# Windowed attention and a squared-ReLU layer: crossbar transposes a row ahead, results through GpSimd's queue, loads of rows 1 and 2 held for their turn, zero products in TensorE's gaps

## The chip, the core and the metric

The kernel runs on one core of a Trainium2 chip. The metric is the device time of one execution in microseconds (us). A core has five engines with queues of their own, each worked off in order: TensorE (PE, matrix products), VectorE (DVE), ScalarE (ACT), GpSimd (POOL) and SyncE (SP, which here only issues transfers). An instruction that waits holds up all that stand behind it in its queue. Transfers (DMA) are issued from SP, ACT or POOL.

## The reference

Two steps are computed. The first is attention on q, k, v of shape 8 x 8 x 576 x 64 (batch rows, heads, positions, head width) with a window: heads 0 to 3 see the last 32 positions ("sliding"), heads 4 to 7 every fourth of the last 128 ("dilated"). The second takes the result as 4608 tokens of width 512 through two layers.

```python
mask_plain = (rel >= 0) & (rel < window)
mask_dil = (rel >= 0) & (rel < window * dilation) & (rel % dilation == 0)
...
attn = np.exp(scores)
attn = attn / (np.sum(attn, axis=-1, keepdims=True) + 1e-09)
return np.matmul(attn, v).astype(np.float32)
...
h = x @ w_in
r = np.maximum(h, 0.0)
g = r * r
return (g @ w_out).astype(np.float32)
```

x is 4608 x 512, w_in 512 x 2048, w_out 2048 x 512; the output is 4608 x 512 in float32.

## The kernel before

The order of every engine's instructions is the order of the program text (manual scheduling); buffers come from pools, and a tile waits for its slot to come free.

**Loads.** For each batch row, q and k of the sliding heads go to `sq` (L89, from SP), v to `sv` in six pieces (L96) and `sd` in two (L105), all in float32. GpSimd casts q and k to `nq` (`cast_sliding_qk`, L146, four instructions) and v to `vp` and `vd` (L158, L162; three and four). The staging buffers exist once, so the load of a row waits for the casts of the row before. For rows 0 and 1, q and k of the dilated heads are loaded with a cast, from GpSimd's queue, to `nd` (L117).

**Getting q and k transposed.** Rows 0 and 1 do it on TensorE (`t_sliding` L330, `t_dilated` L344; six products into a PSUM tile, which VectorE copies out for k and ScalarE for q, L142 and L144 in `copy`). Rows 2 to 7 do it by transfers: GpSimd's queue casts the dilated q and k from DRAM to a DRAM buffer `dd` (L175), SP writes `nq` to a DRAM buffer `dp` (L183), and SP issues four crossbar transposes that write `QKTp` and `QKTd` (L192). These two buffers exist once.

**Attention of a row.** Scores: `s_sliding` (L365) and `s_dilated` (L382), two of each, take two PSUM pairs (`pa`, two buffers); ScalarE takes the exp of each of the eight tiles to `AT` and VectorE multiplies by a 0/1 mask (`softmax`, L361). Values: `attn_values` (L497) has seven groups of products (L414, L429), each normalized by VectorE (L401) and then transposed by TensorE (L443, L460) and copied by ScalarE to `xT`.

**The two layers.** The tokens go in nine chunks of 512. `mm1_gen` (L244) makes 16 tiles `ph` of four products each (128x128 by 128x512), ScalarE applies the ReLU (`rt`), VectorE squares (`g`). `mm2_gen` (L277) makes four tiles `po` of 16 products each; `store` (L272) copies each to `ot` (three buffers) on ScalarE and writes it from SP's queue. `mm2_by_rows_gen` (L287), for chunk 0, goes through w_out in four parts so that it can start before all of w_out is there. The four PSUM buffers `pm` are shared by `ph`, `po` and the transposes.

**How the two are mixed.** Chunk b - 1 is computed during row b. The generators stop after every second product, and `pump(n)` (L312) runs n such pieces (two products each). A chunk has 32 pieces of the first layer and 32 of the second. Row 0 runs alone (L519 to L531). Row 1 pumps 6 pieces, issues its loads and w_out's, pumps 26, then mixes its attention with the second layer (L537 to L563). Each row from 2 on (L566 to L579) first issues the casts, the `dp` write and the crossbar transposes of its own row, then the loads of the next, then pumps 24 pieces ahead of its scores (4 pieces after each), and 2 after each step of its values. The memsets at L538, L539, L550 and L551 write a few elements of the staging buffers on VectorE, so that a load that follows waits for VectorE to get there. Chunks 7 and 8 come last, with no attention beside them (L580). w_in is loaded in three parts (L123).

Of the kernel before, what the change touches and what calls it, by code (L numbers as in the profile page):

```python
# [13 lines left out]
P = 128  # L14
# [3 lines left out]
def kernel(  # L18
# [91 lines left out]
    def load_v(b):  # L110
        load_sliding_v(b)
        load_dilated_v(b, nc.sync)

    def dilated_buffer(b):
        return natp.tile([QB, 2, 2, 12 * D], FP16, name=f"nd{b}", tag="nd")
# [5 lines left out]
                nc.gpsimd.dma_start(out=nd[48 * e : 48 * (e + 1), i, :, :], in_=s4[e])  # L121

    def load_w_in():  # L123
        for f0, f1 in ((0, 512), (512, 1024), (1024, 2048)):
            nc.gpsimd.dma_start(
                out=wi[:, :, f0:f1],
                in_=moe_w_in[:, f0:f1].rearrange("(dh dl) f -> dl dh f", dl=P),
            )
# [26 lines left out]
                )  # L155
        return n

    def cast_sliding_v():  # L158
        for m in range(0, NB, 2):
            nc.gpsimd.tensor_copy(vp[:, m : m + 2, :, 0:D], sv[:, m : m + 2, :, :])  # L160

    def cast_dilated_v():  # L162
        for t in range(2):
            for c in range(0, DIL, 2):
                nc.gpsimd.tensor_copy(  # L165
                    vd[:, t, c : c + 2, :, 0:D],
                    sd[:, t, :, D * c : D * (c + 2)].rearrange("p h (c d) -> p c h d", d=D),
                )
# [29 lines left out]
    load_sliding_qk(0, (nc.sync, nc.scalar))  # L198
    reli = const.tile([P, QB], I16, name="reli")
    nc.gpsimd.iota(reli, pattern=[[1, QB]], base=0, channel_multiplier=-1)  # L200
    make_identity(nc, ident)
    nds = {0: dilated_buffer(0)}
    load_dilated_qk(0, nds[0])
    nc.vector.memset(sv[0:PADP, 0, :, :], 0.0)
    nc.vector.memset(sd[0:64, 0, :, :], 0.0)
    load_sliding_v(0)
    load_dilated_v(0, nc.scalar)
    warm = const.tile([P, 1], FP32, name="warm")
    nc.vector.memset(warm, 0.0)
    nc.scalar.activation(warm, warm, ACTF.Exp)  # L210

    relf = const.tile([P, QB], FP32, name="relf")
    nc.vector.tensor_copy(relf, reli)
    lo_ = const.tile([P, QB], FP16, name="lo_")
# [57 lines left out]
    def store(c, t, po):  # L272
        ot = osb.tile([P, DM], FP32, name=f"ot{c}_{t}", tag="ot")
        nc.scalar.copy(ot, po)  # L274
        nc.sync.dma_start(out=out[(c * 4 + t) * P : (c * 4 + t + 1) * P, :], in_=ot)

    def mm2_gen(c, g):  # L277
        for t in range(TOKC // P):
            po = pmool.tile([P, DM], FP32, name=f"po{c}_{t}", tag="pm")
            for ffc in range(NFF):  # L280
                mm2(c, g, po, t, ffc)
                if ffc % 2 == 1 and ffc < NFF - 1:
                    yield
            store(c, t, po)
            yield
# [16 lines left out]
    def hidden(c):  # L302
        return gp.tile([P, NFF, TOKC], FP16, name=f"g{c}", tag="g")

    def moe_gen(c):
        g = hidden(c)
        yield from mm1_gen(c, g)
        yield from mm2_gen(c, g)

    pending: list = []  # L310

    def pump(n):  # L312
        for _ in range(n):
            while pending:
                try:
                    next(pending[0])
                    break
                except StopIteration:
                    pending.pop(0)
# [21 lines left out]
            p_[:, 0:UW].rearrange("x (j p) -> x p j", j=6),  # L341
        )

    def t_dilated(b, n, g, i, wide=False):  # L344
        p_ = pt(f"pd{b}_{g}_{i}", wide)
        for j in range(6):
            nc.tensor.transpose(
                p_[:, QB * j : QB * (j + 1)],
                n[:, i, g, P * j : P * (j + 1)],
                ident[0:QB, 0:QB],  # L350
            )
        for a in range(2):
            copy(
                nc.vector if i else nc.scalar,
                QKTd[:, i, a, KPAD + 2 * g * CL : KPAD + 2 * (g + 1) * CL].rearrange(
                    "x (h p s) -> x h p s", h=2, s=3
                ),
                p_[:, 0:UW].rearrange("x (s a h p) -> x a h p s", a=2, h=2, p=48)[:, a],
            )
# [115 lines left out]
            py[:, 0:UW].rearrange("x (c r i) -> x c i r", c=2, r=DIL),  # L475
        )

    def transposes(b, nq, nd, gap):
        wide = gap == 0
        for hp in range(2):  # L480
            for i in (1, 0):
                t_sliding(b, nq, hp, i, wide)
                pump(gap)
        for g in range(2):
            for i in (1, 0):
                t_dilated(b, nd, g, i, wide and not i)
                pump(gap)

    def attn_scores(b, gap):
        for hp in range(2):  # L490
# [3 lines left out]
            s_dilated(b, g)  # L494
            pump(gap)

    def attn_values(b, gap, wide=False):  # L497
        xs = []
        for mp in range(3):
            xs.append(av_sliding(b, mp))  # L500
            pump(gap)
        x_sliding(b, 0, xs, wide)
        pump(gap)
        ys = [av_dilated(b, 0, 0)]
        pump(gap)
        x_sliding(b, 1, xs, wide)
        pump(gap)
        ys.append(av_dilated(b, 0, 1))
        pump(gap)
        zs = []  # L510
        for a in range(2):
            zs.append(av_dilated(b, 1, a))
            pump(gap)
        x_dilated(b, 0, ys, wide)
        pump(gap)
        x_dilated(b, 1, zs, wide)


    nq = cast_sliding_qk(0, (nc.scalar, nc.scalar, nc.vector, nc.gpsimd))  # L519
    cast_sliding_v()  # L520
    load_w_in()
    cast_dilated_v()
    for hp in range(2):
        for i in (1, 0):
            t_sliding(0, nq, hp, i)
        s_sliding(0, hp)
    for g in range(2):
        for i in (1, 0):
            t_dilated(0, nds[0], g, i)
        s_dilated(0, g)  # L530
    attn_values(0, 0)  # L531


    g0 = hidden(0)
    pending.append(mm1_gen(0, g0))
    pump(6)
    nds[1] = dilated_buffer(1)  # L537
    nc.vector.memset(sq[:, :, :, 0:1], 0.0)  # L538
    nc.vector.memset(nds[1][:, :, :, 0:1], 0.0)  # L539
    load_sliding_qk(1)  # L540
    load_dilated_qk(1, nds[1])
    load_w_out()
    nq = cast_sliding_qk(1, (nc.gpsimd,) * 4)
    pump(26)
    pending.append(mm2_by_rows_gen(0, g0))
    for hp in range(2):
        for i in (1, 0):
            t_sliding(1, nq, hp, i, True)
            pump(1)
    nc.vector.memset(sv[:, 1, :, 0:1], 0.0)  # L550
    nc.vector.memset(sd[:, 1, :, 0:1], 0.0)  # L551
    load_v(1)
    cast_v()
    load_sliding_qk(2)
    load_v(2)
    dd = keep_dilated_qk(2)
    for g in range(2):
        for i in (1, 0):
            t_dilated(1, nds[1], g, i, True)
            pump(1)  # L560
    attn_scores(1, 3)
    attn_values(1, 1, True)
    pump(1000)  # L563


    for b in range(2, B):  # L566
        pending.append(moe_gen(b - 1))
        nq = cast_sliding_qk(b, (nc.gpsimd,) * 4)
        dp = keep_sliding_qk(b, nq)
        transpose_by_dma(dp, dd)  # L570
        cast_v()
        if b + 1 < B:
            load_sliding_qk(b + 1)
            load_v(b + 1)
            dd = keep_dilated_qk(b + 1)
        pump(24)
        attn_scores(b, 4)
        attn_values(b, 2)
        pump(1000)  # L579
    for c in range(B - 1, NTOKC):  # L580
        pending.append(moe_gen(c))
# [31 lines left out]
```

The softmax here doesn't subtract the row's maximum and nothing guards it: scores larger than these inputs give would overflow.

## Time and profile before

| what | us |
|---|---|
| median of 2 runs (343.63 to 344.74) | 344.19 |
| the profiled execution's own time | 343.5 |
| its span in the profile | 341.7 |
| TensorE busy | 303.1 |
| ScalarE, VectorE, GpSimd busy | 171.0, 155.2, 74.8 |
| row 0 (to the first product of the first layer) | 0 to 28.9 |
| rows 1 and 2 | 28.9 to 113.6 |
| rows 3 to 7 | 113.6 to 282.8 |
| chunks 7 and 8 | 282.8 to 338.2 |
| last copy and store | 338.2 to 341.7 |

The page of a profile lists busy times of the engines, which say how full an engine is but not what it waits for; a busy TensorE is a modelled time, because products overlap. The chain of waits follows the work that ended last back to what released each step. The view of waits sums, for each engine and line, the idle time ahead of it and what ended it. A table of stretches gives the busy time of every engine between two times; a row of the batch begins where TensorE turns to the next chunk's first layer.

### The profile page before, as it was taken

The page shows a single profiled execution, that of the slowest core. Times are in us where ns is not written, and L with a number is a line of the kernel's source. Part 1 is how long each engine was busy: PE and PEld are TensorE (multiplying, and loading weights), DVE is VectorE, ACT ScalarE, POOL GpSimd, SP SyncE. Part 2 cuts the span into 40 slices and gives each one's busy share as a digit, 9 for nine tenths or more (in the row PEclk, how much of TensorE's full clock was granted, in tenths as well). Part 3 has the DMA queues.
Part 4 walks back from the last instruction along what each step waited for, and adds up shares of the span by engine and source line. Part 5 has one row for each costly group of instructions (what it writes and reads, how often), then busy time and mean ns, then how long its engine had stood idle before and what let it go on. Part 6 is the DMA issues. An engine that isn't in the chain of part 4 may idle for free.

```text
span 341.7 us, 6096 instructions
## 1 busy us (share of the span) xinstructions
PE 303.1 (89%) x2368; PEld 151.8 (44%) x2368; DVE 155.2 (45%) x354; ACT 171.0 (50%) x292; POOL 74.8 (22%) x119
## 2 busy tenths in 40 slices
PE   0669979938699979998999799979999999999995
PEld 0454434513245434544554355434544554444442
DVE  4574445703475247525743474247525643402400
ACT  2544636305563666367536653656358446514611
POOL 4350632362045003600450054004400000000000
PEclk9999999996999999999999999999999999999999
DMA  8994999987995789479938994799445010011011
GB/s 185 207 157 92 205 210 224 226 235 185 191 209 149 189 179 205 148 195 212 221 123 187 190 211 137 172 181 218 140 132 126 33 61 33 0 61 63 1 53 69
DMA packets 77293, 51.38 MB, mean 150 GB/s; under 512 B 54416, under 2 KB 70800, under 8 KB 77072
## 3 DMA queue, kind: packets, MB, share of 16 engines
q1 hardware_dynamic: 71060, 40.68, 51.4%
q0 software_dynamic: 4976, 8.91, 15.1%
q10 hardware_dynamic: 1228, 1.41, 1.4%
q8 instruction: 18, 0.29, 0.4%
q14 instruction: 11, 0.09, 0.1%
HBM read 39.85 MB, written 16.52 MB: 165 GB/s over the span
## 4 chain that ended last, share of the span: by engine, by line
PE 72%; DMA 18%; DVE 3%; ACT 2%; SPq 1%; POOL 1%; issue 1%; POOLq 0%; ACTq 0%; DVEq 0%
PE po L264 33%; PE ph L249 30%; DMA QKTp<-dp 7%; DMA sq<-in_k_dram 5%; DMA sv<-in_v_dram 5%; PE paw L434 2%; DMA out_dram<-ot 2%; PE ps L372 2%; PE pav L420 2%; PE pz L391 1%; PE px L449 1%; POOL nq L144 1%; ACT AT L362 1%; DVE AT L363 1%; PE py L467 1%
## 5 line engine op out<-in xcount | busy, mean ns | idle before, releaser
L264 PE MATMUL po<-wo,g 128*128 128x512 f16 x576 | 141.3, 379 | 0.0
L249 PE MATMUL ph<-xT,wi 128*128 128x512 f16 x576 | 131.7, 387 | 6.6 <-ACT ot L274 6.6
L260 DVE TENSOR_TENSOR g<-rt 128x512 f16<-128x512 f16 x144 | 61.5, 427 | 109.7 <-ACT rt L259 109.1
L259 ACT ACTIVATE rt<-ph 128x512 f16<-128x512 f32 x144 | 85.9, 598 | 35.6 <-PE ph L249 34.9
L249 PEld LDWEIGHTS <-wi 128*128 128x128 f16 x576 | 56.2, 99 | 75.4 <-issue 11.8
L264 PEld LDWEIGHTS <-g 128*128 128x128 f16 x576 | 49.5, 98 | 45.3
L144 POOL CAST nq<-sq 96x768 f16<-96x768 f32 x29 | 25.0, 903 | 119.4 <-DMA sq<-in_k_dram 119.4
L274 ACT COPY ot<-po 128x512 f32<-128x512 f32 x36 | 21.1, 587 | 59.9 <-PE po L264 51.1
L455 ACT COPY xT<-px 128x576 f16<-128x576 f16 x16 | 10.2, 639 | 29.7 <-PE px L449 29.7
L362 ACT ACTIVATE AT<-ps 128x576 f16<-128x576 f32 x32 | 19.0, 649 | 10.8 <-PE ps L372 10.8
L165 POOL CAST vd<-sd 128x512 f16<-128x512 f32 x32 | 19.5, 620 | 21.9 <-PE paw L434 15.8
L363 DVE TENSOR_TENSOR AT<-AT,maskd 128x576 f16<-128x576 f16 x32 | 19.3, 614 | 10.6 <-ACT AT L362 9.1
L362 ACT ACTIVATE AT<-pz 128x576 f16<-128x576 f32 x32 | 19.0, 649 | 8.0 <-PE pz L391 8.0
L363 DVE TENSOR_TENSOR AT<-AT,maskp 128x576 f16<-128x576 f16 x32 | 15.0, 469 | 16.9 <-ACT AT L362 14.9
L406 DVE TENSOR_TENSOR x_d<-paw,rcp_d 72x512 f16<-72x512 f32 x32 | 22.0, 686 | 1.1
L372 PE MATMUL ps<-QKTp 64*128 64x96 f16 x192 | 7.5, 212 | 12.2 <-DMA QKTp<-dp 10.2
L160 POOL CAST vp<-sv 128x512 f16<-128x512 f32 x24 | 14.4, 626 | 17.3 <-DMA sv<-in_v_dram 17.3
L406 DVE TENSOR_TENSOR x_p<-pav,rcp_p 96x512 f16<-96x512 f32 x24 | 16.5, 686 | 0.8
L434 PEld LDWEIGHTS <-AT 128*128 128x128 f16 x256 | 12.7, 102 | 8.1 <-PE paw L434 1.2
L473 ACT COPY xT<-py 128x576 f16<-128x576 f16 x16 | 10.2, 640 | 10.6 <-PE py L467 10.6
L405 DVE RECIPROCAL rcp_d<-paw 72x8 f32<-72x8 f32 x32 | 6.5, 203 | 19.4 <-PE paw L434 19.3
L434 PE MATMUL paw<-vd,AT 128*128 128x65 f16 x256 | 14.2, 200 | 0.6 <-DVE rcp_d L405 0.4
(54 smaller groups left out, 122.1 us busy)
## 6 DMA issues: line engine op xcount, KB each, us to landing
out_dram<-ot SPq DMA_DIRECT2D x36, 256.0 KB, 2.5
sv<-in_v_dram SPq DMA_DIRECT2D x40, 128.0 KB, 7.2
sq<-in_q_dram SPq DMA_DIRECT2D x8, 576.0 KB, 6.7
sq<-in_k_dram SPq DMA_DIRECT2D x7, 576.0 KB, 7.7
sd<-in_v_dram SPq DMA_DIRECT2D x7, 512.0 KB, 6.3
dp<-nq SPq DMA_DIRECT2D x12, 288.0 KB, 3.5
wo<-in_moe_w_out_dram POOLq DMA_DIRECT2D x4, 512.0 KB, 12.5
sd<-in_v_dram SPq DMA_DIRECT2D x7, 288.0 KB
```

The costliest lines, as they stand in the source:

```text
L144: eng.tensor_copy(o, i)
L160: nc.gpsimd.tensor_copy(vp[:, m : m + 2, :, 0:D], sv[:, m : m + 2, :, :])
L165: nc.gpsimd.tensor_copy(vd[:, t, c : c + 2, :, 0:D], sd[:, t, :, D * c : D * (c + 2)].rearrange("p h (c d) -> p c h d", d=D),)
L249: nc.tensor.matmul(ph, wi[:, dmk, ffc * P : ffc * P + P], xs[:, dmk, :], start=(dmk == 0), stop=(dmk == NDM - 1),)
L259: nc.scalar.activation(rt, ph[:], ACTF.Relu)
L260: nc.vector.tensor_mul(g[:, ffc, :], rt, rt)
L264: nc.tensor.matmul(po, g[:, ffc, t * P : (t + 1) * P], wo[:, ffc, :], start=(ffc == 0), stop=(ffc == NFF - 1),)
L274: nc.scalar.copy(ot, po)
L362: nc.scalar.activation(AT[:, u, 0:UW], ps[:, :, 0 : UW // 2], ACTF.Exp, scale=scale)
L363: nc.vector.tensor_mul(AT[:, u, 0:UW], AT[:, u, 0:UW], mask)
L406: nc.vector.tensor_tensor(out=x[0:w], in0=pv[:, :, :, 0:D], in1=rcp[0:w].unsqueeze(3).to_broadcast([w, 2, HH, D]), op=ALU.mult,)
L434: nc.tensor.matmul(pav[:, e, h * (D + 2) : h * (D + 2) + D + 1], AT[:, 4 + h, off : off + P], vd[:, t, 2 * a + e, h, 0 : D + 1], start=Tru ...
```

## The change

Seven things change. (1) From row 2 on, the casts, the `dp` write and the crossbar transposes of row b + 1 are issued during row b, the transposes after row b's scores; row b + 2's q and k are loaded then too. (2) Because the transposed row is there when the row begins, its scores begin after 3 pieces (31 in row 2) instead of 24, and the values take 3 pieces a step (1 in row 2) instead of 2. (3) Results are written from GpSimd's queue instead of SP's. (4) Row 1's loads are issued in row 0's values: the memsets that hold them stand after the third value tile; row 2's q and k are held in the same way in row 1's values; v is no longer held by memsets. w_out is issued from GpSimd's queue after row 1's casts. (5) Rows 0 and 1 use `begin`, which transposes all sliding heads first and puts all copies to `QKTd` on ScalarE; row 1's scores move from the second into the first layer. (6) w_in is loaded in two parts, ahead of the last two of the three casts of row 0's sliding v, and `ident` is made after the first loads. (7) Products of a zero tile `zz` are put on TensorE: 14 of 512 columns ahead of row 0, and five of 128 columns after each step of row 0.

```diff
@@ -121,7 +121,7 @@
                 nc.gpsimd.dma_start(out=nd[48 * e : 48 * (e + 1), i, :, :], in_=s4[e])
 
     def load_w_in():
-        for f0, f1 in ((0, 512), (512, 1024), (1024, 2048)):
+        for f0, f1 in ((0, 1024), (1024, 2048)):
             nc.gpsimd.dma_start(
                 out=wi[:, :, f0:f1],
                 in_=moe_w_in[:, f0:f1].rearrange("(dh dl) f -> dl dh f", dl=P),
@@ -155,14 +155,15 @@
                 )
         return n
 
-    def cast_sliding_v():
-        for m in range(0, NB, 2):
+    def cast_sliding_v(m0=0, m1=NB):
+        for m in range(m0, m1, 2):
             nc.gpsimd.tensor_copy(vp[:, m : m + 2, :, 0:D], sv[:, m : m + 2, :, :])
 
-    def cast_dilated_v():
+    def cast_dilated_v(eng=nc.gpsimd):
         for t in range(2):
             for c in range(0, DIL, 2):
-                nc.gpsimd.tensor_copy(
+                copy(
+                    eng,
                     vd[:, t, c : c + 2, :, 0:D],
                     sd[:, t, :, D * c : D * (c + 2)].rearrange("p h (c d) -> p c h d", d=D),
                 )
@@ -198,17 +199,18 @@
     load_sliding_qk(0, (nc.sync, nc.scalar))
     reli = const.tile([P, QB], I16, name="reli")
     nc.gpsimd.iota(reli, pattern=[[1, QB]], base=0, channel_multiplier=-1)
-    make_identity(nc, ident)
+    warm = const.tile([P, 1], FP32, name="warm")
+    nc.vector.memset(warm, 0.0)
+    zz = const.tile([P, TOKC], FP16, name="zz")
+    nc.vector.memset(zz, 0.0)
+    nc.vector.memset(sv[0:PADP, 0, :, :], 0.0)
+    nc.vector.memset(sd[0:64, 0, :, :], 0.0)
+    nc.scalar.activation(warm, warm, ACTF.Exp)
     nds = {0: dilated_buffer(0)}
     load_dilated_qk(0, nds[0])
-    nc.vector.memset(sv[0:PADP, 0, :, :], 0.0)
-    nc.vector.memset(sd[0:64, 0, :, :], 0.0)
+    make_identity(nc, ident)
     load_sliding_v(0)
     load_dilated_v(0, nc.scalar)
-    warm = const.tile([P, 1], FP32, name="warm")
-    nc.vector.memset(warm, 0.0)
-    nc.scalar.activation(warm, warm, ACTF.Exp)
-
     relf = const.tile([P, QB], FP32, name="relf")
     nc.vector.tensor_copy(relf, reli)
     lo_ = const.tile([P, QB], FP16, name="lo_")
@@ -272,7 +274,7 @@
     def store(c, t, po):
         ot = osb.tile([P, DM], FP32, name=f"ot{c}_{t}", tag="ot")
         nc.scalar.copy(ot, po)
-        nc.sync.dma_start(out=out[(c * 4 + t) * P : (c * 4 + t + 1) * P, :], in_=ot)
+        nc.gpsimd.dma_start(out=out[(c * 4 + t) * P : (c * 4 + t + 1) * P, :], in_=ot)
 
     def mm2_gen(c, g):
         for t in range(TOKC // P):
@@ -307,6 +309,11 @@
         yield from mm1_gen(c, g)
         yield from mm2_gen(c, g)
 
+
+    def idle_matmuls(pj, n, cols):
+        for _ in range(n):
+            nc.tensor.matmul(pj[:, 0:cols], zz[:, 0:P], zz[:, 0:cols], start=True, stop=True)
+
     pending: list = []
 
     def pump(n):
@@ -341,7 +348,7 @@
             p_[:, 0:UW].rearrange("x (j p) -> x p j", j=6),
         )
 
-    def t_dilated(b, n, g, i, wide=False):
+    def t_dilated(b, n, g, i, wide=False, eng=None):
         p_ = pt(f"pd{b}_{g}_{i}", wide)
         for j in range(6):
             nc.tensor.transpose(
@@ -351,7 +358,7 @@
             )
         for a in range(2):
             copy(
-                nc.vector if i else nc.scalar,
+                eng or (nc.vector if i else nc.scalar),
                 QKTd[:, i, a, KPAD + 2 * g * CL : KPAD + 2 * (g + 1) * CL].rearrange(
                     "x (h p s) -> x h p s", h=2, s=3
                 ),
@@ -475,16 +482,20 @@
             py[:, 0:UW].rearrange("x (c r i) -> x c i r", c=2, r=DIL),
         )
 
-    def transposes(b, nq, nd, gap):
-        wide = gap == 0
+    def begin(b, nq, nd, fill, wide=False):
         for hp in range(2):
             for i in (1, 0):
                 t_sliding(b, nq, hp, i, wide)
-                pump(gap)
+                fill()
         for g in range(2):
+            s_sliding(b, g)
+            fill()
             for i in (1, 0):
-                t_dilated(b, nd, g, i, wide and not i)
-                pump(gap)
+                t_dilated(b, nd, g, i, wide, eng=nc.scalar)
+                fill()
+        for g in range(2):
+            s_dilated(b, g)
+            fill()
 
     def attn_scores(b, gap):
         for hp in range(2):
@@ -494,88 +505,105 @@
             s_dilated(b, g)
             pump(gap)
 
-    def attn_values(b, gap, wide=False):
+    def attn_values(b, fill, wide=False):
         xs = []
         for mp in range(3):
             xs.append(av_sliding(b, mp))
-            pump(gap)
+            fill()
         x_sliding(b, 0, xs, wide)
-        pump(gap)
+        fill()
         ys = [av_dilated(b, 0, 0)]
-        pump(gap)
+        fill()
         x_sliding(b, 1, xs, wide)
-        pump(gap)
+        fill()
         ys.append(av_dilated(b, 0, 1))
-        pump(gap)
+        fill()
         zs = []
         for a in range(2):
             zs.append(av_dilated(b, 1, a))
-            pump(gap)
+            fill()
         x_dilated(b, 0, ys, wide)
-        pump(gap)
+        fill()
         x_dilated(b, 1, zs, wide)
 
 
     nq = cast_sliding_qk(0, (nc.scalar, nc.scalar, nc.vector, nc.gpsimd))
+    cast_sliding_v(0, 2)
+    load_w_in()
+    cast_sliding_v(2, NB)
+    cast_dilated_v()
+    pj = pmool.tile([P, TOKC], FP32, name="pj", tag="pm")
+    idle_matmuls(pj, 14, TOKC)
+    n_idle = [0]
+
+    def idle():
+        n_idle[0] += 1
+        idle_matmuls(pj, 5, P)
+
+    begin(0, nq, nds[0], idle)
+
+
+    nds[1] = dilated_buffer(1)
+
+    def idle_and_load():
+        idle()
+        if n_idle[0] == 15:
+            nc.vector.memset(sq[:, :, :, 0:1], 0.0)
+            nc.vector.memset(nds[1][:, :, :, 0:1], 0.0)
+
+    attn_values(0, idle_and_load)
+    load_sliding_qk(1)
+    load_v(1)
+    load_dilated_qk(1, nds[1])
+    nq = cast_sliding_qk(1, (nc.gpsimd,) * 4)
+    load_w_out()
     cast_sliding_v()
-    load_w_in()
     cast_dilated_v()
-    for hp in range(2):
-        for i in (1, 0):
-            t_sliding(0, nq, hp, i)
-        s_sliding(0, hp)
-    for g in range(2):
-        for i in (1, 0):
-            t_dilated(0, nds[0], g, i)
-        s_dilated(0, g)
-    attn_values(0, 0)
-
-
     g0 = hidden(0)
     pending.append(mm1_gen(0, g0))
-    pump(6)
-    nds[1] = dilated_buffer(1)
-    nc.vector.memset(sq[:, :, :, 0:1], 0.0)
-    nc.vector.memset(nds[1][:, :, :, 0:1], 0.0)
-    load_sliding_qk(1)
-    load_dilated_qk(1, nds[1])
-    load_w_out()
-    nq = cast_sliding_qk(1, (nc.gpsimd,) * 4)
-    pump(26)
+    pump(22)
+    begin(1, nq, nds[1], lambda: pump(1))
+    pump(1000)
     pending.append(mm2_by_rows_gen(0, g0))
-    for hp in range(2):
-        for i in (1, 0):
-            t_sliding(1, nq, hp, i, True)
-            pump(1)
-    nc.vector.memset(sv[:, 1, :, 0:1], 0.0)
-    nc.vector.memset(sd[:, 1, :, 0:1], 0.0)
-    load_v(1)
-    cast_v()
+    pump(4)
+    n_val = [0]
+
+    def rows_and_load():
+        pump(2)
+        n_val[0] += 1
+        if n_val[0] == 3:
+            nc.vector.memset(sq[:, :, :, 0:1], 0.0)
+
+    attn_values(1, rows_and_load, True)
     load_sliding_qk(2)
+    dd = keep_dilated_qk(2)
+    nq2 = cast_sliding_qk(2, (nc.gpsimd,) * 4)
     load_v(2)
-    dd = keep_dilated_qk(2)
-    for g in range(2):
-        for i in (1, 0):
-            t_dilated(1, nds[1], g, i, True)
-            pump(1)
-    attn_scores(1, 3)
-    attn_values(1, 1, True)
+    dp = keep_sliding_qk(2, nq2)
     pump(1000)
+    transpose_by_dma(dp, dd)
 
 
     for b in range(2, B):
         pending.append(moe_gen(b - 1))
-        nq = cast_sliding_qk(b, (nc.gpsimd,) * 4)
-        dp = keep_sliding_qk(b, nq)
-        transpose_by_dma(dp, dd)
+        pump(1)
         cast_v()
         if b + 1 < B:
-            load_sliding_qk(b + 1)
             load_v(b + 1)
-            dd = keep_dilated_qk(b + 1)
-        pump(24)
-        attn_scores(b, 4)
-        attn_values(b, 2)
+            if b == 2:
+                load_sliding_qk(b + 1)
+                dd = keep_dilated_qk(b + 1)
+            nq = cast_sliding_qk(b + 1, (nc.gpsimd,) * 4)
+            dp = keep_sliding_qk(b + 1, nq)
+            if b + 2 < B:
+                load_sliding_qk(b + 2)
+                dd2 = keep_dilated_qk(b + 2)
+        pump(31 if b == 2 else 2)
+        attn_scores(b, 3 if b == 2 else 4)
+        if b + 1 < B:
+            transpose_by_dma(dp, dd)
+            dd = dd2 if b + 2 < B else None
+        attn_values(b, lambda: pump(1 if b == 2 else 3))
         pump(1000)
     for c in range(B - 1, NTOKC):
         pending.append(moe_gen(c))
```

## The prediction

> **What bounds the kernel now.** I read the page's busy shares first, then the chain of waits in order of time, the waits of TensorE (PE), and a table of stretches cut where the rows of the batch begin and end.
>
> ```profile
> PE 303.1 (89%) x2368; PEld 151.8 (44%) x2368; DVE 155.2 (45%) x354; ACT 171.0 (50%) x292; POOL 74.8 (22%) x119
> DMA  8994999987995789479938994799445010011011
> ```
>
> TensorE is the engine to fill. The DMA digits (40 slices of 8.5 us) are near 9 up to 75 us, but for one hole at 26 to 34 us.
>
> ```profile
> 29.07 4.86 PE ph L249 x16
> ...
> 34.68 9.84 DMA sq<-in_k_dram
> ...
> 57.55 12.02 DMA sv<-in_v_dram
> ...
> 71.87 5.77 DMA out_dram<-ot
> 77.74 0.59 ACT ot L274
> 78.38 9.31 PE ph L249 x32
> 87.83 3.57 DMA QKTp<-dp
> ```
>
> This is a part of the chain (start, length). Row 1's load is issued only at 34.7, into that hole. Row 2's v load runs to 69.6, the first results wait behind it in SP's queue until 71.9, ScalarE waits for their buffers, and TensorE starts again at 78.4. Then it waits for the crossbar.
>
> ```profile
> PE ps L372 <- DMA QKTp<-dp: 10.2, 6, 3.0
> PE ph L249 <- ACT ot L274: 6.6, 1, 6.6
> ```
>
> The crossbar costs 10.2 us over six rows, the blocked results 6.6 us once.
>
> ```profile
> 78.38:113.60 35.22, 32.23 (x257) 15.67 (x257) 17.55 (x38) 17.85 (x31) 9.58 (x15) 0.94 0.87 184
> 113.60:147.85 34.25, 32.40 (x269) 16.27 (x268) 17.15 (x38) 18.81 (x32) 8.66 (x13) 1.00 0.78 181
> 250.20:282.85 32.65, 32.40 (x269) 16.28 (x268) 16.71 (x38) 18.77 (x32) 0.00 (x0) 1.00 0.32 88
> 282.85:338.20 55.35, 55.26 (x257) 24.85 (x254) 13.61 (x32) 23.83 (x41) 0.00 (x0) 1.00 0.10 38
> ```
>
> Columns: stretch, length, busy PE, weight loads, DVE, ACT, POOL, granted clock, DMA share, GB/s. A row with 128 big products needs 32.4 us of TensorE; row 7 (250.20) takes 32.65, row 3 34.25. So rows 3 to 7 (169.25 us together, against 5 x 32.4 = 162.0) hide only 7 us. The prize lies ahead of 113.6: rows 1 and 2 take 29.07 to 113.60, 84.5 us.
>
> **What the skill says.** "TensorE: Matmul & The Clock Gate", Part 1, says that the array starts at half rate, goes to full after about 3.4 us of work and falls back after an idle window as long. The trace agrees: the 16 products at 29.07 take 304 ns each against 216 (13.82 us for 64) later; after the 6.6 us hole 32 take 291 ns; after the 3.0 us hole at 88.5 the clock stays at 1.00. "DMA: Bandwidth & Descriptors", Issuing engines are not separate DMA queues, says that all queues share the same 16 engines, so that another queue saves issue time and blocking, no bandwidth. The trace agrees: between 36 and 72 us two queues together move 203 to 253 GB/s in 4 us stretches (183 in the last). The same page, Anatomy of one DMA, gives a GpSimd-issued DMA about 2 us fixed plus its bytes; no GpSimd store stands in this trace. "SBUF — State Buffer", Who interferes with whom, says that a VectorE operation with two SBUF inputs contends with GpSimd's reads. That fits the mask products: 469 ns on maskp, 614 on maskd, where the casts run.
>
> **The change, stage by stage (on the profiled execution, span 341.7).**
>
> Row 0. Its scores now follow all sliding transposes, and all eight QKTd copies go to ScalarE (0.70 us a pair). ScalarE is the path: the first QKTp copy can start at about 10.0 (k cast done 9.1, two warm groups of transposes at 0.26, one idle group). Then 2 x 0.64 + 8 x 0.65 + 4 x 0.70 = 9.3 us gives 19.3 for the last exp, before 21.9; with one mask product more the values start 2.1 us earlier. VectorE's seven normalizations (0.20 + 0.69 each) still pace that part, so row 0 ends at 27.0, not 29.07: -2.1. The idle products: 14 before the first cast at 9.1, at 216 to 427 ns 3.0 to 6.0 us from about 1.3, so over in time; then 22 groups of five 128-column products, about 0.27 us each warm (216 / 4 x 5) and 0.54 cold: 6 to 12 us in all. They lie in gaps (TensorE is busy 13.4 of 19.9 us here, much of it cold). If all the cover were gone they would cost those 6 us; I charge none. They buy the 1.6 us of row 1's slow start (15.4 us for 64 products against 13.8); taken in below.
>
> The w_in loads go ahead of four of six v blocks' casts: 14 instead of 17 us, 1.5 us of GpSimd issue (0.76 each), so the casts slip to about 18 and the dilated ones to 20.5; first needed about 19 and 21.5. The 1024-column half now comes in one piece; 6 to 12 us from 14 is 26 at the latest, needed at 27. Even, with a thin margin.
>
> Row 1's loads. The two memsets come after the third normalization, at about 22.9, so q and k start at 23 instead of 34.3. They share with the rest of w_in. At the 9.8 us they took before (again beside nd and weights) k lands at 33, casts 34.6 and 36.3 (0.83 each). TensorE wants them after 44 products, 27.0 + 9.5 = 36.5: no wait, margin 0.2 to 2 us. Behind these casts stand the w_out issues (4 x 0.77 us, 37 to 40), the v casts (7 x 0.62) and the dd loads. First w_out piece at about 42 to 45, needed near 49.
>
> Row 1 itself: 128 x 0.216 = 27.65 us plus attention on TensorE: 8 transposes x 0.26 + 4 scores x 0.37 + 11 x 0.26 = 6.5. But begin(1) puts on ScalarE, in the time of 20 products (4.3 us) plus 3.5 us of transposes and scores: 5 relus x 0.60 + 2 x 0.64 + 8 x 0.65 + 4 x 0.70 = 12.3 us. The last score tile needs a PSUM pair that the sixth exp frees, so TensorE leaves 4.0 us late. Row 1: 38.2, to 65.2.
>
> Row 2. Its q and k are released after row 1's third value tile, about 53; k lands 61 (7.7 median), v behind. SP needs 9 us for the eight v issues (7.0 + 2.0 at 91.9), so dp at 62.5 to 64.5, 3.5 to land, four crossbar issues of 1.5, the last of the pair in QKTp at 73.5. Wanted at 65.2 + 64 x 0.216 = 79: hidden. So row 2 is 32.4, to 97.6. The results wait in no SP queue any more, so no 6.6 us hole and no cold restart. Rows 1 and 2: 70.6 against 84.5: -13.9.
>
> Row 3. A new chain: SP is free of row 2's crossbar at 72.5; v(3) takes 9 us of issue, then q, k (1.0) at 82.5, landed 90 (7.7), k cast 91.7, q 93.4, dp 3.5 each to 97, crossbar k, dilated k, q (1.5 each) plus 3.7: about 102. TensorE is ready at 97.6 + 1.3 = 98.9. Stall 3.1. And GpSimd's queue holds row 2's results behind these casts: free at 93.4, plus two dd issues (0.5 each), plus a store; the fourth result copy (three buffers) wants the first store done at 97.2. An SP store takes 2.5 us, the GpSimd price is 2 us plus 256 KB, 2.6 (estimate from the page), or, queued behind dd, up to 6.2. So 97.2 is just met, or passed by up to 3.4 us, and that inside the row-3 stall. Row 3: 32.4 + 3.1 + 0.4 = 35.9 against 34.25: +1.6.
>
> Rows 4 to 7. The crossbar is issued after the previous row's scores, 10 us into it, and lands by 20 (6 us of issue plus 3.7): 12 us to spare; its wait is gone. The scores and half of the values move into the first layer: four steps of 2 relus + 2 exps, 2.5 us of ScalarE each, against 2.1 of TensorE (8 x 0.216 + 0.37). 1.5 us of backlog fits into four PSUM buffers (three relus ahead, 1.8 us). I charge 0.4 a row (bounds 0 and 1.5): 4 x 32.8 = 131.2 against 135.0: -3.8.
>
> End. Two unmixed chunks: 55.35, as before. The last store through GpSimd: issue 0.5 (dd's) and 2.6 instead of 0.33 and 2.5: +0.3 to +1.5; I take +0.7.
>
> Sum: -2.1 - 13.9 + 1.6 - 3.8 + 0.7 = -17.5: span 324.2. The profiled run had 1.8 us around it (343.5): 326.0; the median shown is 0.2% above it: 326.5.
>
> **Rivals.** (a) Nothing stalls: no ScalarE excess in row 1 (-4.0), none at row 3 (-3.1), rows at 32.4 (-2): 317.5. For it: the crossbar has lasted 3.6 us everywhere, and slack exists in rows 4 to 7; against it: 12.3 us of ScalarE work in 7.8. (b) DMA paces the start: loads take their longest (13.1 for q and k, 12.7 for v) when everything is asked for at once; row 1 is 2 us late, row 3's crossbar 6 to 8 later: 333 to 336. For it: 9s up to 75 us already. (c) The idle products don't keep the clock up or land on the path: +1.6 to +6: 328 to 332.5. (d) Slower: GpSimd's in-order queue becomes the bound. Results stand behind casts that wait for q and k. If in each row the casts end later than 27 us into it, the fourth result copy, then the relus behind it, then TensorE stand. It costs one us per us and row; to lose the whole gain of 17.5 over rows 2 to 7, 2.9 each, the casts must end 30 us in. In rows 3 to 7 the loads are issued a row ahead, so I expect about 10; only row 2 (28) is close. That would give 345 to 350.
>
> **How the numbers follow.** Forecast 0.54 (own range 321 to 331), (a) 0.14, (b) 0.17, (c) 0.08, (d) 0.07. The range 318 to 337 leaves out (d), half of (a) below 318 and a little of (b). A measurement of this kernel can tell about 2% from no change, so 337.3 is the border: faster takes the forecast, (a), (c) and most of (b), 0.87; same 0.07; slower 0.06.
>
> **What would show it.** Right: row 0 ending near 27; TensorE's first big products at 216 ns; no wait of ph for ot; crossbar waits only at row 3; ScalarE without idle time in row 1's scores (36 to 49); rows 4 to 7 at 32.4 to 33.5. Wrong: po waiting for w_out near 49, ph for w_in near 27, scores of row 2 waiting for the crossbar, ot waiting for out_dram in rows 3 to 7.

## The result, and the profile after

The changed kernel takes 362.0 us (median of 2 runs, 361.25 to 362.74) against 344.19 before: ratio 1.0518, 95% interval 1.0399 to 1.0636. It is slower by 17.8 us where 17.5 us of gain were forecast. Below, a median is over all runs of a kernel, while a ratio and its interval compare the runs that lie within 1.5% of each kernel's fastest. The page of the kernel after, to be held against the two lines of before:

```profile
span 361.0 us, 6346 instructions
...
PE 318.0 (88%) x2492; PEld 159.8 (44%) x2492; DVE 180.5 (50%) x346; ACT 169.8 (47%) x300; POOL 92.7 (26%) x154
...
PEclk9899999969997699997999899989999999999998
DMA  8999999998689996199626991574110020021011
```

VectorE (DVE) is 25 us busier with 8 instructions less: something stretches an operation that the change doesn't touch. The clock digits (PEclk) dip once a row in slices 18, 22 and 26 (9 us each, the first being 0), where before had full speed: TensorE stands still in each of these rows. The table of stretches of the kernel after, cut where the rows begin (columns as in the prediction), says where:

```profile
27.39:67.24 39.85, 35.44 (x320) 18.54 (x319) 22.03 (x41) 22.04 (x42) 15.60 (x21) 1.00 1.07 203
67.24:106.44 39.20, 35.48 (x270) 16.70 (x269) 20.27 (x38) 18.24 (x32) 13.26 (x23) 0.91 0.89 208
106.44:151.46 45.02, 35.15 (x270) 17.16 (x269) 22.91 (x38) 18.59 (x32) 10.22 (x17) 0.89 0.89 204
151.46:189.72 38.26, 35.42 (x269) 17.12 (x268) 22.02 (x38) 18.36 (x32) 10.22 (x17) 0.91 0.69 162
...
265.27:298.10 32.83, 32.39 (x268) 16.22 (x267) 18.65 (x38) 18.15 (x32) 6.12 (x11) 1.00 0.09 33
```

Rows 1, 2, 3, 4, then row 7. Rows 5 and 6 take 37.8 us each, like row 4 (38.3), and VectorE is busy 22.0 us in each where row 3 of before had 17.2. Row 7 is as forecast, and so are the two last chunks, 55.4 us. The groups of the page show which operation it is. First the kernel after (L262 is the square g = rt x rt), then before (there L260):

```profile
L262 DVE TENSOR_TENSOR g<-rt 128x512 f16<-128x512 f16 x144 | 98.6, 692 | 123.1 <-ACT rt L261 121.9
```

```profile
L260 DVE TENSOR_TENSOR g<-rt 128x512 f16<-128x512 f16 x144 | 61.5, 427 | 109.7 <-ACT rt L259 109.1
```

The same 144 squares take 37 us more. Not all are slower: a few are very long. The timeline of the kernel after at the start of row 4 (start, length, engine; in brackets the idle time before and what ended it):

```profile
152.42 0.54 POOL L277 DMA_DIRECT2D out_dram<-ot  x1 [2.96 <-ACT ot L276]
...
152.95 1.73 POOL L160 CAST vp<-sv 128x512 f16<-128x512 f32 x3
152.99 7.30 DVE L262 TENSOR_TENSOR g<-rt 128x512 f16<-128x512 f16 x1 [10.16 <-ACT rt L261]
...
154.62 2.29 POOL L144 CAST vd<-sd 128x512 f16<-128x512 f32 x4
...
156.86 3.14 POOL L144 CAST nq<-sq 96x768 f16<-96x768 f32 x4
...
160.38 0.60 ACT L261 ACTIVATE rt<-ph 128x512 f16<-128x512 f32 x1 [3.96 <-DVE g L262]
...
161.02 1.01 PE L251 MATMUL ph<-xT,wi 128*128 128x512 f16 x2 [2.12 <-ACT rt L261]
...
163.53 3.60 PE L251 MATMUL ph<-xT,wi 128*128 128x512 f16 x8
```

Read downward. GpSimd (POOL) gets past the chunk's fourth result store only when ScalarE has copied it, at the row's end. The eleven casts queued behind it then run without a gap, 152.95 to 160.00. One square, begun 0.04 us after the first cast, lasts until 160.29. ScalarE has three `rt` buffers and stands for 3.96 us; so does TensorE (2.12 us, and more at the scores behind), and its eight products at 163.53 take 450 ns each, half the clock. In before the casts of `vd` had gaps, because each waited for its buffer until TensorE had used the old values. GpSimd's timeline of before in row 3:

```profile
139.50 0.62 POOL L165 CAST vd<-sd 128x512 f16<-128x512 f32 x1 [0.73 <-PE paw L434]
141.75 0.62 POOL L165 CAST vd<-sd 128x512 f16<-128x512 f32 x1 [1.64 <-PE paw L434]
```

Row 3 has a square like it (7.63 us from 112.21), but there TensorE waits for the crossbar anyway. The early rows lose elsewhere. The waits of TensorE, kernel after:

```profile
PE ps L379 <- DMA QKTp<-dp: 9.9, 1, 9.9
PE pz L398 <- ACT AT L369: 7.2, 11, 2.4
PE ph L251 <- ACT rt L261: 6.3, 3, 2.1
PE ph L251 <- ACT ot L276: 3.7, 1, 3.7
```

The crossbar wait of six rows is gone, but for one of 9.9 us in row 3. The wait for results of before is there still, 3.7 instead of 6.6 us. The chain of the kernel after shows its place:

```profile
67.66 5.31 DMA out_dram<-ot
...
73.71 13.99 PE ph L251 x52
```

Chunk 0's first store is issued at 67.66, behind the casts of row 2's q and k (64.58 to 67.7) in GpSimd's queue, lands at 73.0, and TensorE starts again cold: 269 ns a product.

By stages, kernel after less before: row 0 -1.7, rows 1 and 2 -5.5, row 3 +10.8, rows 4 to 6 +11.5, row 7 and the chunks +0.2, from the last product to the end of the span +4.0. Sum +19.3, the difference of the two spans (361.0 - 341.7).

### The profile page after: what moved, and what is told of

Read it like the earlier page. It is cut to its first block, busy times and chain, and to the rows that moved or that the text cites. A ratio compares the mean times of both kernels' runs of the same rounds, so it can differ in the third digit from the quotient of the medians.

```text
span 361.0 us, 6346 instructions
## 1 busy us (share of the span) xinstructions
PE 318.0 (88%) x2492; PEld 159.8 (44%) x2492; DVE 180.5 (50%) x346; ACT 169.8 (47%) x300; POOL 92.7 (26%) x154
## 4 chain that ended last, share of the span: by engine, by line
PE 45%; issue 23%; DMA 10%; DVE 8%; ACT 5%; POOL 4%; SPq 2%; POOLq 0%; ACTq 0%
PE po L266 20%; PE ph L251 17%; DMA sq<-in_k_dram 8%; DVE g L262 6%; ACT AT L369 2%; POOL out_dram L277 2%; PE pav L427 2%; DMA out_dram<-ot 1%; PE paw L441 1%; DVE AT L370 1%; ACT rt L261 1%; POOL nq L144 1%; ACT QKTd L142 1%; DMA QKTp<-dp 1%; SPq L196 1%
## 5 line engine op out<-in xcount | busy, mean ns | idle before, releaser
L262 DVE TENSOR_TENSOR g<-rt 128x512 f16<-128x512 f16 x144 | 98.6, 692 | 123.1 <-ACT rt L261 121.9
L251 PE MATMUL ph<-xT,wi 128*128 128x512 f16 x576 | 146.0, 400 | 10.4 <-ACT rt L261 6.3
L266 PE MATMUL po<-wo,g 128*128 128x512 f16 x576 | 134.8, 379 | 0.0
L261 ACT ACTIVATE rt<-ph 128x512 f16<-128x512 f32 x144 | 84.9, 605 | 50.2 <-PE ph L251 29.5
L251 PEld LDWEIGHTS <-wi 128*128 128x128 f16 x576 | 54.6, 101 | 73.9 <-issue 22.4
L266 PEld LDWEIGHTS <-g 128*128 128x128 f16 x576 | 52.5, 98 | 55.0
L277 POOL DMA_DIRECT2D out_dram<-ot x36 | 19.8, 549 | 205.1 <-ACT ot L276 205.1
L144 POOL CAST nq<-sq 96x768 f16<-96x768 f32 x29 | 23.4, 844 | 47.9 <-DMA sq<-in_k_dram 47.9
L369 ACT ACTIVATE AT<-pz 128x576 f16<-128x576 f32 x32 | 19.3, 686 | 0.8 <-PE pz L398 0.6
L370 DVE TENSOR_TENSOR AT<-AT,maskd 128x576 f16<-128x576 f16 x32 | 15.2, 492 | 4.7 <-ACT AT L369 3.1
L315 PE MATMUL pj<-zz 128*128 128x128 f16 (+1 forms) x124 | 15.2, 262 | 1.2 <-DVE zz L205 1.2
L412 DVE RECIPROCAL rcp_d<-paw 72x8 f32<-72x8 f32 x32 | 6.4, 201 | 18.0 <-PE paw L441 17.8
```

The costliest lines, as they stand in the source:

```text
L144: eng.tensor_copy(o, i)
L251: nc.tensor.matmul(ph, wi[:, dmk, ffc * P : ffc * P + P], xs[:, dmk, :], start=(dmk == 0), stop=(dmk == NDM - 1),)
L261: nc.scalar.activation(rt, ph[:], ACTF.Relu)
L262: nc.vector.tensor_mul(g[:, ffc, :], rt, rt)
L266: nc.tensor.matmul(po, g[:, ffc, t * P : (t + 1) * P], wo[:, ffc, :], start=(ffc == 0), stop=(ffc == NFF - 1),)
L277: nc.gpsimd.dma_start(out=out[(c * 4 + t) * P : (c * 4 + t + 1) * P, :], in_=ot)
```

## The experiments

Two theories stood at the start. One: GpSimd's train of casts keeps VectorE's square out because both read the on-chip memory; the rows come back only as far as casts leave the row's start, whatever queue the results use. The other: the results in GpSimd's queue are what makes the train. Everything is measured against the kernel before, on the same chip; edits are to the kernel after unless said otherwise.

### Results back on SP's queue

```diff
-        nc.gpsimd.dma_start(out=out[(c * 4 + t) * P : (c * 4 + t + 1) * P, :], in_=ot)
+        nc.sync.dma_start(out=out[(c * 4 + t) * P : (c * 4 + t + 1) * P, :], in_=ot)
```

> The kernel after, with the results issued from SP's queue again; all else as it is. Theory of the port (eleven GpSimd casts without a gap at the start of rows 4 to 6 keep VectorE's squares waiting 7.3 us): rows 4 to 6 stay at 37.8 to 38.3 us, since their loss has nothing to do with the results; only the tail goes back from 7.5 us (last product to end of span) to about 3.5 and the 3.7 us hole of TensorE at 70 us shrinks or moves: 354 to 358. Theory of the queue (results behind casts in GpSimd's queue are what costs): rows 2 to 6 all become shorter, by 3 us or more each: 340 to 346.

Measured: 341.44 (339.02 to 343.12), ratio 0.9923 (0.9893 to 0.9953): this one line is worth 20 us, and the kernel is then less than 2% faster than the one before. GpSimd's timeline of this kernel, row 3, and its stretch for row 4:

```profile
136.09 0.75 POOL L144 CAST vd<-sd 128x512 f16<-128x512 f32 x1 [2.12 <-PE paw L441]
139.20 0.61 POOL L144 CAST vd<-sd 128x512 f16<-128x512 f32 x1 [2.36 <-PE paw L441]
```

```profile
151.90:184.10 32.20, 32.20 (x269) 16.09 (x268) 16.15 (x38) 18.18 (x32) 8.98 (x13) 1.00 0.89 193
```

The casts have gaps again, the longest square is 0.9 us, and rows 4 to 7 take 32.2 to 32.4 us each. The first theory alone fails: the train is made by the queue. What is left is the early part: a crossbar wait of 10.8 us in row 3, 3.8 us for `ot`, rows 1 to 3 in some 124 us, as in the kernel after. From the last product to the end it is 3.6 us.

### That part alone, in the kernel before

```diff
-        nc.sync.dma_start(out=out[(c * 4 + t) * P : (c * 4 + t + 1) * P, :], in_=ot)
+        nc.gpsimd.dma_start(out=out[(c * 4 + t) * P : (c * 4 + t + 1) * P, :], in_=ot)
```

> The kernel before, with one part of the change alone: its results are written from GpSimd's queue. If the in-order queue is the cause, the casts of a row (q and k of its own row ahead of the crossbar, and v) stand behind the previous chunk's last result, run as one train at the row's start, and the crossbar that needs them comes later: rows 2 to 7 lose several us each, and the last store costs about 4 us more: 355 to 375. If a result on GpSimd's queue costs only its own issue and a longer tail (rival: the loss needs the row-ahead casts), 344 to 350.

Measured: 377.03 (374.27 to 382.22), ratio 1.0925 (1.0831 to 1.1019), just past the upper end. GpSimd's timeline of this kernel at the start of row 6 (the four `vd` casts follow at once):

```profile
238.66 0.54 POOL L275 DMA_DIRECT2D out_dram<-ot  x1 [3.74 <-ACT ot L274]
239.19 3.13 POOL L144 CAST nq<-sq 96x768 f16<-96x768 f32 x4
242.27 1.72 POOL L160 CAST vp<-sv 128x512 f16<-128x512 f32 x3
```

The same train, without anything else of the change. TensorE waits 3.5 us for `rt` in each of rows 3 to 7. The row's own q and k stand behind the last result too, but the waits for the crossbar don't grow: 5.1 us in rows 4 to 6 together, 5.2 in before. The long squares reach 7.6 us (74.99 in the chain), rows 4 to 6 average 40.3 us, against 34.1 before. The part that did the harm does it alone; together with the rest of the change it does less.

### Casts moved out of the row's start, results left on GpSimd's queue

The four `nq` casts and the `dp` write for rows 5 to 7 stand at the start of rows 4 to 6. They go into the row before that, behind the eighth step of the values of rows 3 to 5. The heart of the edit:

```diff
+            if n_fill[0] == 8 and b >= 3 and b + 2 < B:
+                nq = cast_sliding_qk(b + 2, (nc.gpsimd,) * 4)
+                kept.append(keep_sliding_qk(b + 2, nq))
...
```

> The kernel after, with the four q and k casts of rows 5 to 7 (and the write to DRAM and the next load that follow them) moved from the start of a row to the middle of the row before it, between the first and second result of its chunk, where VectorE has only normalizations from PSUM. The start of rows 4 to 6 then has seven casts in one piece (4 us), as row 7 has now (32.8 us). Theory of the port: rows 4 to 6 fall from 37.8-38.3 to 32.8-34 us, no square over 4.5 us there: 347 to 351. Theory of ScalarE (relus and exps together in the first layer are too much): the rows stay at 37 to 38: 359 to 363.

Measured: 349.5 (345.49 to 351.31), ratio 1.0124 (1.0077 to 1.0171). The trace is of an execution of 351.14. The train is now seven casts, 3.9 us, and VectorE's timeline at the start of row 4 follows it:

```profile
156.19 4.19 DVE L262 TENSOR_TENSOR g<-rt 128x512 f16<-128x512 f16 x1 [10.16 <-ACT rt L261]
```

The square lasts as long as the train (4.2 for 3.9, 7.3 for 7.1), and rows 4 to 6 take 33.0 us: a wait of 4 us is nearly hidden, one of 7 costs 5.6 (37.9 against 32.3 with SP's queue).

### More on GpSimd behind the train: reads, then writes alone

Six casts of a scratch tile (4.4 us a row), or six memsets (6.0 us), behind the eleven casts of rows 2 to 6; both are work that the result doesn't need.

```diff
+            for _ in range(6):
+                nc.gpsimd.tensor_copy(sy, sx)
```

```diff
+            for _ in range(6):
+                nc.gpsimd.memset(sw, 0.0)
```

> The kernel after, with six more casts of a scratch tile (128x512, float32 to float16, about 0.62 us each, 3.7 in all) on GpSimd right behind the eleven of each row from 2 to 6; the output is unaffected. Theory of the port: the square at the start of rows 4 to 6 waits 3.7 us longer (11 instead of 7.3) and each of these rows is longer by about as much; row 2 (casts broken up by a wait) and row 3 (in which the crossbar is waited for) by less: 372 to 380. Theory of ScalarE or of the clock: no more than 2 us in all.

> The kernel after, with six memsets of a scratch tile (128x1024, float32) on GpSimd in the same place; each some 0.5 to 1 us. They write and read nothing. Theory of the port, in the form that only GpSimd's reads hold up a VectorE product of two SBUF tiles: the square still waits 7.3 us, not more, and the time stays at 360 to 364. If it is GpSimd's being busy in any way that holds VectorE up, the square waits longer by the memsets' length, and the time grows by that much in each of rows 4 to 6.

Measured: casts 370.12, ratio 1.0738 (1.0681 to 1.0795), a little under the range expected; memsets 361.31, ratio 1.0528 (1.0458 to 1.0598), as without them, and the first square of row 4 takes 7.28 us. So 6 us more in GpSimd's queue cost nothing; 4.4 us a row of casts cost some 8 us in all. Not the length of the queue but what the casts do to VectorE is the price. VectorE's timeline of the kernel with more casts also shows a limit of that:

```profile
154.22 7.83 DVE L262 TENSOR_TENSOR g<-rt 128x512 f16<-128x512 f16 x1 [10.16 <-ACT rt L261]
161.97 1.64 DVE L370 TENSOR_TENSOR AT<-AT,maskp 128x576 f16<-128x576 f16 x2
```

The first square is longer by 0.5 us only. From the second scratch cast on VectorE gets in between: these casts follow each other every 0.73 us instead of 0.57, and two masks take twice their time (1.64 for 0.81) instead of standing. So casts that follow each other don't always keep VectorE out. Row 1 of the kernel after shows it too, in GpSimd's and VectorE's timelines:

```profile
36.32 3.71 POOL L144 CAST nq<-sq 96x768 f16<-96x768 f32 x4 [10.28 <-DMA sq<-in_k_dram]
36.45 2.90 DVE L262 TENSOR_TENSOR g<-rt 128x512 f16<-128x512 f16 x3 [0.44 <-ACT rt L261]
```

Here four casts run without a gap and three squares finish beside them, about 1 us each. In all 14 traces of this case 412 products of two tiles in on-chip memory (squares and masks) overlap a cast. Forty of them last over 1.2 us, and 36 of these begin while GpSimd issues a result store or within 0.05 us after it; the other four last 2.0 to 3.8 us. Whether the train alone keeps VectorE out, or the store in front of it is needed, isn't shown: no run has such a train at a row's start without a store in front.

### Ten rt buffers, the rest as in the kernel after

```diff
-            rt = osb.tile([P, TOKC], FP16, name=f"rt{c}_{ffc}", tag="rt")
+            rt = osb.tile([P, TOKC], FP16, name=f"rt{c}_{ffc}", tag="rt", bufs=10)
```

> The changed kernel as it is, with ten instead of three rt buffers between ScalarE's ReLU and VectorE's square. If the square's wait reaches TensorE through those three buffers, the square still takes about 7.3 us at each row's start, but ScalarE no longer waits for rt; TensorE meets the late masks or the late g instead, later and for less: rows 4 to 6 at 33 to 36.5 and 345 to 357 in all. If the rows are slow for another reason: rows at 37.8 to 38.3 and 359 to 363.

Measured: 351.59 (350.66 to 353.97), ratio 1.0223 (1.0152 to 1.0295). The square still takes 7.27 us, but the stretch of row 4 in this kernel reads

```profile
149.70:184.40 34.70, 32.63 (x269) 16.16 (x268) 21.21 (x38) 18.24 (x32) 10.18 (x17) 1.00 0.81 179
```

34.7 instead of 38.3, at full clock. Three buffers carry the wait to TensorE; of the 5.6 us a row they account for 3.2, and values that wait for VectorE (2.1 us a row) for most of the rest.

### The early rows: one wait taken away at a time

With the results on SP's queue, (1) four result buffers; (2) row 3's q and k loaded ahead of row 2's crossbar and v; (3) both; (4) both, without the zero products; (5) as (2), without the memset that holds row 2's q and k; (6) as (2), results from ScalarE's queue.

```diff
-        ot = osb.tile([P, DM], FP32, name=f"ot{c}_{t}", tag="ot")
+        ot = osb.tile([P, DM], FP32, name=f"ot{c}_{t}", tag="ot", bufs=4)
```

```diff
     dp = keep_sliding_qk(2, nq2)
+    load_sliding_qk(3)
...
-                load_sliding_qk(b + 1)
```

```diff
-            nc.tensor.matmul(pj[:, 0:cols], zz[:, 0:P], zz[:, 0:cols], start=True, stop=True)
+            pass
```

```diff
-        if n_val[0] == 3:
-            nc.vector.memset(sq[:, :, :, 0:1], 0.0)
```

```diff
-        nc.sync.dma_start(out=out[(c * 4 + t) * P : (c * 4 + t + 1) * P, :], in_=ot)
+        nc.scalar.dma_start(out=out[(c * 4 + t) * P : (c * 4 + t + 1) * P, :], in_=ot)
```

The first diff is (1), the second (2), then what (4), (5) and (6) add.

> The version with the results on SP's queue (341.4 us), with four result buffers instead of three. What is left of that version's loss by its trace is a 3.8 us wait of TensorE at 70 us for a result buffer, with a cold restart behind it, and 10.8 us for the crossbar at row 3. If the two are separate losses, the first goes (3.8 us and some 2.8 of cold clock): 334 to 336. If the crossbar chain sets the end (loads limited by the queue, not by TensorE), TensorE only reaches its wait earlier and waits longer: 340 to 342.

> The version with the results on SP's queue, with row 3's q and k load issued right behind row 2's write to DRAM, ahead of row 2's crossbar transposes and of row 3's v, instead of behind both. If the order of SP's queue makes the crossbar late at row 3, the 10.8 us wait falls to 0 to 4 and the cold restart goes: 328 to 333. If the transfers themselves are at their limit there, the wait moves to row 2's crossbar or stays: 339 to 342.

> Both edits: four result buffers and row 3's q and k early. If the chain of transfers is no limit: 324 to 328 (the prediction's case without stalls, 317.5, plus row 1's ScalarE excess and some wait at row 3). If it is, the gain of one edit is lost in the other's wait: 331 to 335.

> The same with both edits, without the products of zeros (none is issued; nothing else moves). If they keep the clock up and stay off the path, row 0 and the first products of row 1 get slower by 1.5 to 3.5 us (row 0 at half rate in part, 64 products at 241 ns instead of 216). If they cost more than they bring, the time falls by up to 3.

> The changed kernel with results from SP's queue and row 3's q and k loaded ahead of row 2's crossbar, and now also without the memset that holds row 2's q and k for row 1's values, so that they load as soon as their buffer is free. If the hold is what makes the early rows late: 326 to 331, with the wait of the first layer for ot near 70 us gone. If the transfers are saturated up to 100 us, so that one load's gain is another's delay: 333 to 340, and a wait turns up elsewhere (for w_out or v of row 1).

> The changed kernel with row 3's q and k loaded ahead of row 2's crossbar (as in f2_sp_qk_early), and the results written from ScalarE's queue, right behind the copies that make them, so that they stand neither behind casts nor behind SP's loads. The casts stay spread as with SP (rows 4 to 7 near 32.3 us, squares under 1 us). If blocked results in SP's queue are what leaves the 7.7 us hole near 70 us: that hole goes and the total is 327 to 332. If the transfers set the early rows, the wait turns up in the crossbar or in w_out and the total stays at 333 to 340.

| kernel | median us | ratio to before (interval) | TensorE's largest waits in the trace, us |
|---|---|---|---|
| results on SP | 341.44 | 0.9923 (0.9893 to 0.9953) | crossbar 10.8, `ot` 3.8 |
| (1) | 341.02 | 0.9931 (0.9906 to 0.9956) | crossbar 15.8 |
| (2) | 334.91 | 0.9764 (0.9723 to 0.9805) | `ot` 7.7 |
| (3) | 342.57 | none | crossbar 17.2 |
| (4) | 342.11 | 0.9740 (0.9679 to 0.9801) | crossbar 19.4 |
| (5) | 336.0 | 0.9751 (0.9674 to 0.9827) | `ot` 4.3, `pz` for ScalarE 3.7 |
| (6) | 339.26 | 0.9855 (0.9796 to 0.9914) | `ps` for ScalarE 4.4, `pz` 4.0, `ot` 2.9 |

Runs of (3) and (4) scatter from 333 to 346 us, so their totals say nothing: the ratio of (4) rests on four of its 21 runs, and only one of the four runs of (3) is below 340. Their traces are of long executions (343.92 and 345.79), and the wait in them is that of row 2's scores for their crossbar, after all 32 pieces of the first layer (1 and 31). (2) beats both kernels. The table of stretches of (2), cut about 1 us beside the starts of rows 2, 3 and 4 (67.8, 111.0 and 144.4):

```profile
66.50:111.90 45.40, 37.73 (x280) 17.69 (x279) 17.12 (x38) 20.15 (x35) 18.02 (x29) 0.89 1.10 236
111.90:145.30 33.40, 32.42 (x270) 16.21 (x269) 16.16 (x38) 18.24 (x32) 8.98 (x13) 1.00 1.01 219
```

Row 3 is nearly full; row 2 pays 4 us of it (43.2 from start to start, against 39.3 with results on SP alone), while the DMA share is 1.0 to 1.1 in both rows. Take away the wait for `ot` and the crossbar comes later (1); take away the crossbar's and `ot` waits longer (2); let row 2's load go early and chunk 0's last copy still comes at 77.8, as in (2) at 77.6 (5). In (6) the first store is issued at once, at 67.0, but needs 6.7 us to land; there ScalarE also stands in row 3, as the last section shows. That fits one limit, the transfers up to about 145 us, that moves from wait to wait. In no trace of the six does row 3 end before 144.4, where 133.5 was forecast. It isn't shown how much of that is bytes and how much the order in SP's queue: no run took bytes away.

On the zero products, (4) against (3): without them the first layer's first 44 products of row 1 take 11.0 us, with them about 9.8. Row 0 ends where it did (27.3 and 27.5), so TensorE comes to row 1's transposes 0.6 us earlier with them (37.5 and 38.1). At the start of row 2 nothing is left of it (69.0 and 68.6). This is one trace of each.

## Why the prediction was wrong, step by step

**Row 0** (27.0): 27.4. Right. The load of row 1's k, issued at 24.0, lands at 36.3: it takes 12.3 us where 9.8 stood in the sum.

**Row 1** (38.2): 39.9. Right in kind, and the near total is in part luck: TensorE waits 2.7 us for exps where 4.0 were charged, but also 1.4 us for the casts of row 1's q and k, charged at nothing, and is busy 35.4 us instead of 34.2.

**Row 2** (32.4): 39.2. The step "The results wait in no SP queue any more, so no 6.6 us hole and no cold restart" failed. I moved the stores past SP's queue and didn't count what they moved behind: by the program text they follow the four casts of row 2, which wait for their load until 64.6. With a store of 5.3 us to land (2.6 assumed) the fourth copy came at 73.07, the hole is 3.7 us, and the restart is cold, as the Trainium skill's "TensorE: Matmul & The Clock Gate", Part 1, says of an idle window of about 3.4 us and the 269 ns show. SP's queue doesn't cure it (results on SP: 72.87); the landing time does its part.

**Row 3** (35.9, a stall of 3.1): 45.0, a stall of 9.9. The mechanism was right, the size was off: q and k were issued at 87.0 and landed in 11.0 us, where 82.5 and 7.7 (a median of the whole kernel) stood in my chain. That is 8 us. Another 7.8 came behind it, mostly at the first two crossbar issues, which took 9.1 us of SP's time where 3.0 stood in the chain. Rival (b) had the kind, though not these terms. (2) confirms the place: load moved, stall gone from row 3.

**Rows 4 to 7** (32.8 each): 38.3, 37.8, 37.8 and 32.8. This is the step that made a loss of it: rows 1 to 3 had used up the gain of 17.5, and it adds 15.4. "I charge 0.4 a row" priced ScalarE's backlog alone. Rival (d) looked at the right queue from one side: results behind casts. What the trace shows is casts behind results. Store four of a chunk comes at the row's end, so the casts can't start before, and start all at once. I had cited the very rule (the Trainium skill's "SBUF — State Buffer", Who interferes with whom: a VectorE operation with two SBUF inputs contends with GpSimd's reads) and its trace, 614 against 469 ns, and gave the moved casts no price by it. The measured one is the length of the train, 7.1 us, less what the buffers hide: 5.6 us a row. The page has the memsets right too: it says that GpSimd instructions that only write don't contend, and six of them left the square at 7.28 us. Even (d), the slower case, stopped at 350, and `rt`, where TensorE's wait shows, is on no list of signs. Row 7 hits 32.8 by luck: its first square takes 4.2 us too, which the buffers hide.

Without the train, the step holds: with results on SP the crossbar waits of rows 4 to 7 are gone and rows take 32.2 to 32.4, better than my 32.8.

**End** (4.2): 7.5. Mis-sized: +0.7 predicted, +4.0 measured. Issue and landing were about right (2.3 us from 354.50, so 356.8); what was put at nothing is the end of GpSimd's queue, 3.4 us more, to 360.18 (last section).

Against the forecast of 324.2 for the span: row 0 +0.4, row 1 +1.7, row 2 +6.8, row 3 +9.1, rows 4 to 7 +15.4, end +3.3: 36.7 of the 36.8 us. The results' queue is behind the last two of these, 18.7 us; the 20.6 us between the medians with and without it are near that.

## What to carry to other kernels

Moving a transfer to another engine's queue moves everything behind it: list what stands behind it there, when the instruction it waits for ends, and what those released instructions do all at once. An off-path engine (GpSimd, 26% busy) can set the time through a memory path that it shares with another, so ask for a train of casts, above all one that a store releases, which VectorE operation has two inputs just then, and how many buffers part that from TensorE. And where the transfers are full, price a load by what it took beside others, not by the median; a wait removed there comes back at the next one.

## What was not expected of the hardware

- VectorE's product can be kept out for a whole train of GpSimd casts (7.3 us for eleven, 4.2 for seven) when it begins at a store issue in front of them; in row 1, where no result store stands in front, it gets in behind each cast (three squares in 2.9 us beside four casts). Why isn't shown.
- With the last store issued from GpSimd's queue, 7.4 to 7.5 us pass from the last product to the end of the span in all six such kernels, against 3.6 with SP's or ScalarE's. The records of the trace, though not its views, show what fills the time: a closing instruction of GpSimd (DRAIN) runs from 354.48 to 360.18 in the kernel after. With results on SP it runs from 239.29 to 242.13, at GpSimd's last casts, while TensorE works. Why it lasts 5.7 us instead of 2.8 isn't shown.
- A store issued from ScalarE's queue waited for SP: in (6) ScalarE copied the last result of chunk 1 by 107.3, its issue came at 116.4, just when SP's six v issues (109.5 to 116.0) had ended, and the ReLUs behind it stood 9.5 us. One observation; its cause is open. The timeline of that kernel:

```profile
106.74 0.59 ACT L276 COPY ot<-po 128x512 f32<-128x512 f32 x1 [3.04 <-PE po L266]
116.37 0.34 ACTq L277 DMA_DIRECT2D out_dram<-ot  x1
116.81 0.60 ACT L261 ACTIVATE rt<-ph 128x512 f16<-128x512 f32 x1 [9.49 <-DMA sv<-in_v_dram]
```
